# Attention and eight experts on one core: the rows beyond 512 of each expert as 64-column products inside the long ones, 64 more behind one branch, output transfers without an order between them

## The chip, the cores and the metric

One core of a Trainium2 chip runs the whole program in one launch. The metric is device time in microseconds (us): the median of the runs, each of them the time of one launch. Engines are named as in the profile: PE (TensorE matmul) and PEld (its weight loads), DVE (VectorE), ACT (ScalarE), POOL (GpSimd), SP (SyncE, which issues transfers).

## What is computed

Causal attention with a decay bias over 8 x 8 heads (576 positions, head size 64), and behind it a layer of eight experts with top-1 routing over the 8 x 576 = 4608 rows of 512 values that the attention leaves:

```python
scores = scale * q @ k.T + np.minimum(-(cum[:, None] - cum[None, :]), 0.0)   # causal
x = softmax(scores) @ v                       # per head, laid out as (4608, 512)
logits = (x / |x|) @ (emb / |emb|).T / tau
expert_idx = np.argmax(logits, axis=1)
for e in range(8):
    mask = expert_idx == e
    h = np.maximum(x[mask] @ w1[e], 0.0)      # 512 -> 1024
    out[mask] = gate_w[mask, None] * (h @ w2[e])   # 1024 -> 512
```

How many rows an expert has is known only on the chip; the mean is 576. Products are made from f16 pairs (a high and a low part), three products for one: high x high, high x low, low x high.

## The kernel before

The attention is laid out by hand in steps `step(n)` and ends some 395 us into the span; what the change touches comes after. Every engine runs its instructions in the order in which the program writes them (`manual_schedule`), so the code's order is the order of each queue.

Rows are routed by an indirect scatter into one list for each expert (`xs` in DRAM); an expert handles up to 640 of them here (`CAP`), in five tiles of 128. `MAIN` is 512 (four tiles), `HALF` is 576. Rows beyond 640 go to the loop `overflow`, which a count on the chip turns 0 times where there are none.

An expert e is worked off in two layers (the loop from line 1235 on):

- Layer 1, `l1(m, e, 0, MAIN)` for eight blocks m of 128 hidden units: 12 products of 512 columns each (`l1mm`, line 830; four parts c of the 512 inputs, three pairs k of high and low) into a tile `pxs` in PSUM, of which there are two, taken in turn. `hsplit` (lines 835 and 836) then makes the f16 pair: ACT writes the high part, DVE the low one.
- The tail of layer 1, `l1tail` (line 865): the fifth tile of rows. `cases` (line 859) writes two blocks of PE instructions, one behind "over 576 rows" (96 products of 128 columns) and one behind "513 to 576 rows" (96 products of 64 columns). Both write the PSUM tile `T`, and one `hsplit` over 128 x 1024 values follows.
- Layer 2, `l2(e, t)` for the four full tiles t: 24 products of 512 columns (line 913) into a `pxs`, then `put` (line 918): DVE scales the result into one of three slots of `Kx` (line 921), and POOL scatters it to `out` with an indirect transfer (line 922). In the last expert the last tile goes to the tile `om` instead (`l2h`) and is written behind the overflow loop (lines 1389 to 1391).
- The tail of layer 2, `l2tail` (line 876), third of the five turns t of the loop: again two blocks. Over 576 rows: 24 products of 512 columns into `Y` (line 880). From 513 to 576: 96 products of 64 columns with the weights as the loaded operand, whose result stands turned in `yT` (line 886). ACT copies `yT` to a slot of `Kx` (line 889). In the fifth turn `l2tail_out` (line 891) turns it back by four transposes behind a third branch, and `put` scatters `Y`.

Beside this, ACT and DVE convert the next weights (`wcv`: lines 814 and 822; `wsq`, line 786, takes their squares; `wnorm`, lines 797 to 804, makes the scale, with one product of 8 columns on PE), POOL gathers the next rows (`xload`, line 713), and `xprep` (lines 744 to 753) turns them: for experts 0 and 1 by four PE transposes (line 746) into the single PSUM tile `pxm`, which ACT (line 751) and DVE (line 753) read; from expert 2 on by transfers from SP.

Expert 0 is special: 384 of its rows are done early, its tiles 3 and 4 in two halves `hb` of four blocks each, and the rows of expert 1 are prepared between. `count1` loads an expert's row count into PE registers for the branches, twice in each expert (one for each case).

The output transfers all write `out`, so each waits until the one before has landed.

Of the kernel before, what the change touches and what calls it, by code (L numbers as in the profile page):

```python
# [12 lines left out]
I32 = mybir.dt.int32  # L13
# [96 lines left out]
def main(ctx, tc, qkh, qkc, vtin, s_in, emb, tau, w1h, w2h, out, shared, nb):  # L110
# [98 lines left out]
    def setup4():  # L209
# [14 lines left out]
        IX["e0"], IX["nf"], IX["ni"] = t[:, 470:470 + NE], t[:, 478:478 + NE], t[:, 486:486 + 2 * NE].bitcast(I32)  # L224
# [355 lines left out]
    def router(b, xt):  # L580
# [57 lines left out]
        def rows():  # L638
# [4 lines left out]
            nc.vector.tensor_copy(IX["ni"][:, 0:NE], IX["nf"])  # L643
            nc.vector.scalar_tensor_tensor(IX["ni"][:, NE:2 * NE], IX["nf"], float(HALF), IX["nf"], op0=ALU.is_le, op1=ALU.mult)
# [201 lines left out]
    def count1(e):  # L846
        for k in range(2):
            X[("n", e, k)] = nc.values_load(IX["ni"][0:1, NE * k + e:NE * k + e + 1], engines=[mybir.EngineType.PE], min_val=0, max_val=NT,
                                            skip_runtime_bounds_check_because="it is a count of the 4608 rows")

    def tails():
        ta, tb = (ps_t.tile([128, 2, 512], F32, tag="t", name=f"T{i}") for i in range(2))
        HT["T"] = ta.rearrange("p b (m t) -> p (b m) t", t=128)
        HT["Y"], HT["yT"] = tb[:, 0], tb[:, 1].rearrange("p (d t) -> p d t", d=4)
        z = PLs[0][:, 1600:1664].unsqueeze(1).to_broadcast([128, 8, 64])
        for o in (ta[:, 0], ta[:, 1], tb[:, 0], tb[:, 1]):
# [15 lines left out]
    def prods(m, e):  # L872
        (wH, wL), (hH, hL) = wt(2, m), (X[("T", e)][:, k, m] for k in range(2))
        return [(hH, wH, m == 0, False), (hL, wH, False, False), (hH, wL, False, m == 7)]

    def l2tail(e):
        def direct():
            for m in range(8):
                for h, w, a, z in prods(m, e):
                    nc.tensor.matmul(HT["Y"], h, w, start=a, stop=z)  # L880

        def turned():
            for d in range(4):
                for m in range(8):
                    for h, w, a, z in prods(m, e):
                        nc.tensor.matmul(HT["yT"][:, d, 0:64], w[:, 128 * d:128 * d + 128], h[:, 0:64], start=a, stop=z)
        cases(e, direct, turned)
        X[("y", e)] = yslot()[:, 0:256].rearrange("p (d t) -> p d t", d=4)
        nc.scalar.copy(X[("y", e)], HT["yT"][:, :, 0:64])

    def l2tail_out(e):
        with tc.If(X[("n", e, 1)] > MAIN):
            for d in range(4):
                nc.tensor.transpose(out=HT["Y"][0:64, 128 * d:128 * d + 128], in_=X[("y", e)][:, d], identity=ident)
        put(e, NTL - 1, HT["Y"])
# [5 lines left out]
    def l2h(e, t):  # L901
        for m in range(8):
            (wH, wL), (hH, hL) = wt(2, m), htile(m)
            for k, (h, w) in enumerate(((hH, wH), (hL, wH), (hH, wL))):
                nc.tensor.matmul(om, h[:, 128 * t:128 * t + 128], w, start=(m == 0 and k == 0), stop=(m == 7 and k == 2))

    def l2(e, t, mid={}):
# [517 lines left out]
```

## Time and profile before

| | |
|---|---|
| median of 3 runs | 789.34 us (787.21 to 792.22) |
| the profiled execution's own time | 790.14 us |
| span of its profile, first to last instruction | 788.0 us |
| mean granted PE clock | 0.989 of full |
| PE / ACT / DVE / POOL busy | 753.6 / 569.0 / 525.1 / 385.7 us |

A span is measured on the core itself; the execution's own time lies 2.1 us above it. In the profile a PE product's shown duration holds its way through the array as well, and products overlap: what one costs is the distance from its start to the start of the next. "Idle before" is the time in which an engine did nothing before an instruction, with what ended it; PEq is PE's sequencer, which runs the branches.

### The profile page before, as it was taken

The page shows a single profiled execution, that of the slowest core. Times are in us where ns is not written, and L with a number is a line of the kernel's source. Part 1 is how long each engine was busy: PE and PEld are TensorE (multiplying, and loading weights), DVE is VectorE, ACT ScalarE, POOL GpSimd, SP SyncE. Part 2 cuts the span into 40 slices and gives each one's busy share as a digit, 9 for nine tenths or more (in the row PEclk, how much of TensorE's full clock was granted, in tenths as well). Part 3 has the DMA queues.
Part 4 walks back from the last instruction along what each step waited for, and adds up shares of the span by engine and source line. Part 5 has one row for each costly group of instructions (what it writes and reads, how often), then busy time and mean ns, then how long its engine had stood idle before and what let it go on. Part 6 is the DMA issues. An engine that isn't in the chain of part 4 may idle for free. (4 is left out here: it accounts for less than half of the span.)

```text
span 788.0 us, 20375 instructions
## 1 busy us (share of the span) xinstructions
PE 753.6 (96%) x7694; PEld 537.2 (68%) x7694; DVE 525.1 (67%) x1789; ACT 569.0 (72%) x1020; POOL 385.7 (49%) x370
## 2 busy tenths in 40 slices
PE   8799999999999999998899999999999999999995
PEld 4599999999999999985465555545445555454452
DVE  7667888888888888877657757555575566644611
ACT  6689989999999998975638778647648586574500
POOL 8667798989898979771432112131131122211001
PEclk9899999999999999999999999999999999999998
DMA  8997879898979796780625756545555567642001
GB/s 157 193 196 134 177 177 208 179 204 181 203 177 210 175 209 152 183 280 20 225 77 177 190 169 193 144 147 163 144 197 133 148 195 172 207 98 79 15 28 42
DMA packets 76910, 125.26 MB, mean 159 GB/s; under 512 B 38960, under 2 KB 39364, under 8 KB 75934
## 3 DMA queue, kind: packets, MB, share of 16 engines
q0 software_dynamic: 20240, 70.92, 38.4%
q1 hardware_dynamic: 56560, 52.84, 24.7%
q8 instruction: 72, 1.18, 0.6%
q14 instruction: 38, 0.31, 0.1%
HBM read 95.23 MB, written 21.49 MB: 148 GB/s over the span
## 5 line engine op out<-in xcount | busy, mean ns | idle before, releaser
L240 POOL TENSOR_TENSOR PL<-P 128x576 f16<-128x576 f32 (+2 forms) x128 | 203.5, 1695 | 18.6 <-ACT P L483 10.5
L830 PEld LDWEIGHTS <-wt 128*128 128x128 f16 x1632 | 113.5, 98 | 93.7 <-issue 9.8
L922 POOL DMA_INDIRECT out<-Kx,xj x39 | 43.4, 1112 | 204.7 <-DVE Kx L921 153.2
L830 PE MATMUL pxs<-xH,wt 128*128 128x512 f16 (+1 forms) x512 | 141.6, 359 | 0.6 <-DVE hq L836 0.2
L511 PE MATMUL om<-vh,P 128*128 128x73 f16 x960 | 107.6, 199 | 3.4 <-DVE xt L536 3.0
L513 PE MATMUL om<-vh,PL 128*128 128x73 f16 x960 | 106.9, 198 | 0.5 <-POOL PL L240 0.5
L512 PE MATMUL om<-vl,P 128*128 128x72 f16 x960 | 107.0, 197 | 0.0
L348 PE MATMUL s<-qkb 96*128 96x288 f32 (+4 forms) x270 | 97.7, 375 | 1.6 <-DVE M L356 0.9
L512 PEld LDWEIGHTS <-P 128*128 128x128 bf16 x960 | 95.1, 99 | 4.5 <-issue 4.1
L513 PEld LDWEIGHTS <-PL 128*128 128x128 f16 x960 | 94.2, 98 | 0.6 <-POOL PL L240 0.6
L511 PEld LDWEIGHTS <-P 128*128 128x128 bf16 x960 | 94.1, 99 | 0.2
L713 POOL DMA_INDIRECT Qx<-xs,idx x40 | 43.2, 1080 | 102.9 <-ACT vjunk L786 50.9
L830 PE MATMUL pxs<-xL,wt 128*128 128x512 f16 (+1 forms) x256 | 90.3, 359 | 0.0
L356 DVE CUSTOM_DVE_ANT_0 junk<-s,mS 128x320 bf16<-128x320 f32 (+3 forms) x142 | 73.3, 524 | 4.9 <-PE s L348 3.5
L913 PE MATMUL pxs<-wt,hp 128*128 128x512 f16 x270 | 73.0, 379 | 0.0
L913 PE MATMUL pxs<-wt,hq 128*128 128x512 f16 x270 | 68.2, 379 | 0.0
L486 ACT ACTIVATE P<-tb 128x1024 f32<-128x1024 f32 x64 | 65.2, 1019 | 3.4 <-PE tb L453 2.3
L822 DVE SCALAR_TENSOR_TENSOR wt<-ring,idx,wt 128x512 f16<-128x512 f32 x80 | 56.8, 746 | 14.3 <-ACT wt L814 14.2
L921 DVE TENSOR_SCALAR Kx<-pxs,xj,idx 128x512 f32<-128x512 f32 x31 | 25.1, 810 | 61.6 <-PE pxs L913 37.0
L450 PE MATMUL tb<-QC,KC 128*128 128x448 f32 (+3 forms) x256 | 64.1, 309 | 0.0
L814 ACT ACTIVATE wt<-ring,idx 128x512 f16<-128x512 f32 x80 | 53.5, 711 | 14.0 <-DVE idx L801 14.0
L483 ACT ACTIVATE P<-ta 128x576 f32<-128x576 f32 x64 | 41.2, 644 | 28.2 <-PE ta L450 26.5
(268 smaller groups left out, 1903.0 us busy)
## 6 DMA issues: line engine op xcount, KB each, us to landing
qkb<-qkh POOLq DMA_DIRECT2D x15, 1216.0 KB, 9.3
ring<-w2h SPq DMA_DIRECT2D x44, 256.0 KB
ring<-w1h SPq DMA_DIRECT2D x36, 256.0 KB
vT<-vtin SPq DMA_DIRECT2D x28, 320.0 KB
KC<-qkh POOLq DMA_DIRECT2D x15, 576.0 KB, 8.9
QC<-qkh POOLq DMA_DIRECT2D x15, 576.0 KB, 8.1
rw<-w1h SPq DMA_DIRECT2D x15, 256.0 KB
rw<-w2h SPq DMA_DIRECT2D x12, 256.0 KB
```

The lines of the kernel that those rows point to most:

```text
L240: nc.gpsimd.tensor_tensor(out, a, b_, op=ALU.subtract)
L348: nc.tensor.matmul(out, G[g]["QB"][0:96, h, 128 * i:128 * i + 128], G[g]["KB"][0:96, h, lo:hi], start=True, stop=True)
L356: nc.vector.tensor_tensor_reduce(out=jk, in0=src, in1=ms, scale=1.0, scalar=NEG, op0=ALU.add, op1=ALU.max, accum_out=MP[n // 2][:, n % 2, ...
L450: nc.tensor.matmul(out, HD[n]["KC"][:, ks:ks + 128], HD[n]["QC"][:, qlo:qhi], start=False, stop=stop)
L486: nc.scalar.activation(HD[n]["P32"][:, 576:1600], HD[n]["tb"], AF.Exp, scale=0.125)
L511: nc.tensor.matmul(out, lh, vh[:, kb], start=(kb == 0), stop=False)
L512: nc.tensor.matmul(out[:, u:u + 72], lh, vl[:, kb], start=False, stop=False)
L513: nc.tensor.matmul(out, ll, vh[:, kb], start=False, stop=(kb == j))
L814: nc.scalar.activation(h, a, AF.Copy, scale=s)
L822: nc.vector.scalar_tensor_tensor(l, a, s, h, op0=ALU.mult, op1=ALU.subtract)
L830: nc.tensor.matmul(h, w[:, 128 * c:128 * c + 128], x[:, c, lo:hi], start=(c == 0 and k == 0), stop=(c == 3 and k == 2))
L913: nc.tensor.matmul(y, h, w, start=(m == 0 and k == 0), stop=(m == 7 and k == 2))
```

## The change

Expert by expert the fifth tile is split at row 576. The 64 rows from 512 on are always done: in layer 1 each 512-column product is followed by a 64-column product with the same weights into `T`; in layer 2 the turned products (12 of 64 columns) follow each block m of the second turn. The 64 rows from 576 on stand behind one branch in each layer (96 products of 64 columns each). The turned result is 128 columns wide for every expert, and four transposes bring it back into a `pxs`, without a branch. In expert 0, where there is no such turn, the eight groups of turned products follow `l2(0, 3)`; the transposes of expert 1's rows 3 and 4 move to other places of `l2(0, 3)`. The count is loaded once. The output transfers are declared independent of one another.

```diff
-    def l1mm(h, m, e, lo, hi, mid=None):
+    def l1mm(h, m, e, lo, hi, mid=None, tail=False):
...
-                nc.tensor.matmul(h, w[:, 128 * c:128 * c + 128], x[:, c, lo:hi], start=(c == 0 and k == 0), stop=(c == 3 and k == 2))
+                for o, a, b in ((h, lo, hi), (HT["T"][:, m, 0:64], MAIN, HALF)) if tail else ((h, lo, hi),):
+                    nc.tensor.matmul(o, w[:, 128 * c:128 * c + 128], x[:, c, a:b], start=(c == 0 and k == 0), stop=(c == 3 and k == 2))
...
-        l1mm(h, m, e, lo, hi, mid)
+        l1mm(h, m, e, lo, hi, mid, e > 0)
...
-    def cases(e, both, one):
-        with tc.If(X[("n", e, 0)] > HALF):
-            both()
-        with tc.If(X[("n", e, 1)] > MAIN):
-            one()
-
     def l1tail(e):
-        def go(n):
+        with tc.If(X[("n", e)] > HALF):
             for m in range(8):
-                l1mm(HT["T"][:, m, 0:n], m, e, MAIN, MAIN + n)
-        cases(e, partial(go, 128), partial(go, 64))
+                l1mm(HT["T"][:, m, 64:128], m, e, HALF, CAP)
         hsplit(*(X[("T", e)][:, k] for k in range(2)), HT["T"])
...
+    def turned(e, m, lo):
+        for d in range(4):
+            for h, w, a, z in prods(m, e, "T"):
+                nc.tensor.matmul(HT["yT"][:, d, lo:lo + 64], w[:, 128 * d:128 * d + 128], h[:, lo:lo + 64], start=a and d == 0, stop=z and d == 3)
+
     def l2tail(e):
...
-        cases(e, direct, turned)
-        X[("y", e)] = yslot()[:, 0:256].rearrange("p (d t) -> p d t", d=4)
-        nc.scalar.copy(X[("y", e)], HT["yT"][:, :, 0:64])
+        with tc.If(X[("n", e)] > HALF):
+            for m in range(8):
+                turned(e, m, 64)
+        X[("y", e)] = yslot()
+        nc.scalar.copy(X[("y", e)].rearrange("p (d t) -> p d t", d=4), HT["yT"])
 
     def l2tail_out(e):
-        with tc.If(X[("n", e, 1)] > MAIN):
-            for d in range(4):
-                nc.tensor.transpose(out=HT["Y"][0:64, 128 * d:128 * d + 128], in_=X[("y", e)][:, d], identity=ident)
-        put(e, NTL - 1, HT["Y"])
+        y = pxs()
+        for d in range(4):
+            nc.tensor.transpose(out=y[:, 128 * d:128 * d + 128], in_=X[("y", e)][:, 128 * d:128 * d + 128], identity=ident)
+        put(e, NTL - 1, y)
...
+            if tail:
+                turned(e, m, 0)
...
+    puts = []
...
+        for o in puts:
+            tc.declare_no_dep(ins, o, reason="a token is a row of one tile, so the tiles write distinct rows")
+        puts.append(ins)
...
-            l1mm(hb[:, m % 4], m, 0, SPL, MAIN)
+            l1mm(hb[:, m % 4], m, 0, SPL, MAIN, tail=True)
...
-    l2(0, 3, {3: lambda: xprep(1, 3, pxm())})
+    l2(0, 3, {1: lambda: xprep(1, 3, pxm()), 6: lambda: xprep(1, 4, pxm())})
...
+    for m in range(8):
+        turned(0, m, 0)
     l2tail(0)
...
                 l2tail_out(0)
-                xprep(1, 4, pxm())
...
-            if t == 4:
-                l2tail_out(e)
             if t == 2:
                 l2tail(e)
+            elif t == 4:
+                l2tail_out(e)
+                (l2 if nx else l2h)(e, LAST)
             else:
-                (l2 if nx or t < 4 else l2h)(e, t - (t > 2))
+                l2(e, t - (t > 2), tail=(t == 1))
```

Three places show what this does to the queues. The first is PE in the fifth turn of expert 2, between the end of layer 2's tile 2 and the start of tile 3 (`hv` is a block of hidden values, `Kx` the copied turned result, `om` the product of `wnorm`; what an instruction waits for stands in brackets).

```order
L913 MATMUL pxs<-wt,hv 128x512
L797 LDWEIGHTS onesb [waits DVE_49]
L797 MATMUL om<-idx,onesb 128x8 [waits Activation_49]
L892 COMPARE_AND_BRANCH
L894 MATMUL T_7484<-ident,Kx 64x128 x4
L892 UNCONDITIONAL_BRANCH
L892 UNCONDITIONAL_BRANCH [waits PE_49]
L913 LDWEIGHTS hv
L913 MATMUL pxs<-wt,hv 128x512 [waits DVE_49]
```

```order
L905 MATMUL pxs<-wt,hv 128x512
L796 LDWEIGHTS onesb [waits DVE_49]
L796 MATMUL om<-idx,onesb 128x8 [waits Activation_49]
L889 MATMUL pxs<-ident,Kx 128x128 [waits DVE_49]
L889 MATMUL pxs<-ident,Kx 128x128 x3
L905 LDWEIGHTS hv
L905 MATMUL pxs<-wt,hv 128x512 [waits DVE_49]
```

Above is before, below after: the branch is gone, and the transposes now write a `pxs`, so that one tile of the two is taken between two long products.

The second is PE in `l2(0, 3)` of expert 0, where rows of expert 1 are turned into `pxm` (`Qx` are gathered rows; of runs of equal rows the first or last is shown).

```order
L797 MATMUL om<-idx,onesb 128x8
L913 LDWEIGHTS xH [waits Activation_49]
...
L913 MATMUL pxs<-wt,xH 128x512
L746 MATMUL pxm<-ident,Qx 128x128 [waits DMASW0_49,DVE_49]
L746 MATMUL pxm<-ident,Qx 128x128 x3
L913 LDWEIGHTS xH [waits Activation_49]
...
L913 MATMUL pxs<-wt,xH 128x512
L860 COMPARE_AND_BRANCH
```

```order
L796 MATMUL om<-idx,onesb 128x8
L905 LDWEIGHTS xH [waits Activation_49]
...
L745 MATMUL pxm<-ident,Qx 128x128 [waits DMASW0_49,DVE_49]
L745 MATMUL pxm<-ident,Qx 128x128 x3
...
L905 LDWEIGHTS xH [waits Activation_49]
...
L745 MATMUL pxm<-ident,Qx 128x128 [waits DMASW1_49,DVE_49]
L745 MATMUL pxm<-ident,Qx 128x128 x3
...
L877 MATMUL yT<-xH,wt 128x64 [waits Activation_49]
```

Before, four transposes stand behind 12 of the 24 long products; after, four behind 6 of them and four more behind 21, and both groups write the one tile `pxm`.

The third is POOL's queue at the end of the program, the last expert's four output transfers.

```order
L922 DMA out<-Kx,xj 4608x512 [waits DMASW7_49,DMASW0_49,DVE_49]
...
L922 DMA out<-Kx,xj 4608x512 [waits DMASW1_49,DMASW0_49,DVE_49]
...
L922 DMA out<-Kx,xj 4608x512 [waits DMASW2_49,DMASW1_49,DVE_49]
L922 DMA out<-Kx,xj 4608x512 [waits DMASW2_49,DVE_49]
L1318 COMPARE_AND_BRANCH
L1318 ISA [waits DMASW4_49,DMASW5_49,DMASW3_49,DMASW6_49,DMASW2_49,DMASW7_49,DMASW1_49,DMASW0_49]
```

```order
L918 DMA out<-Kx,xj 4608x512 [waits DMASW0_49,DVE_49]
...
L918 DMA out<-Kx,xj 4608x512 [waits DMASW1_49,DVE_49]
L918 DMA out<-Kx,xj 4608x512 [waits DMASW2_49,DVE_49]
L918 DMA out<-Kx,xj 4608x512 [waits DMASW3_49,DVE_49]
L1319 COMPARE_AND_BRANCH
L1319 ISA [waits DMASW4_49,DMASW5_49,DMASW3_49,DMASW6_49,DMASW2_49,DMASW7_49,DMASW1_49,DMASW0_49]
```

The wait for the transfer just before (DMASW0, DMASW1, DMASW2) is gone; the wait for all transfers ahead of the overflow loop stays.

## Rows read from the trace of the kernel before

**Rows 1.** The page, part 1: busy time of each engine, its share of the span and its instructions.

```profile
PE 753.6 (96%) x7694; PEld 537.2 (68%) x7694; DVE 525.1 (67%) x1789; ACT 569.0 (72%) x1020; POOL 385.7 (49%) x370
```

**Rows 2.** Busy time by stage: from the second part of expert 0, experts 3 and 4 (columns: the stretch in us, its length, then busy us and instructions of PE, PEld, DVE, ACT and POOL, granted PE clock, DMA share, GB/s).

```profile
395.50:421.40 25.90, 23.53 (x356) 17.44 (x354) 15.21 (x46) 14.36 (x34) 7.17 (x7) 1.00 0.34 108
...
521.90:575.10 53.20, 52.67 (x316) 26.45 (x315) 29.82 (x74) 33.44 (x78) 11.18 (x10) 1.00 0.53 155
575.10:623.85 48.75, 48.02 (x392) 24.68 (x391) 29.87 (x74) 33.28 (x78) 11.46 (x10) 1.00 0.64 172
```

**Rows 3.** PE in order of time in layer 2 of expert 4 (start us, us, instruction, count, idle before and its releaser).

```profile
604.52 0.17 PE L797 MATMUL om<-idx,onesb 128*128 128x8 bf16 x1
604.55 0.81 PE L913 MATMUL pxs<-wt,hv 128*128 128x512 f16 x3
...
609.08 0.81 PE L913 MATMUL pxs<-wt,hv 128*128 128x512 f16 x3
610.21 2.97 PE L886 MATMUL T<-xH,wt 128*128 128x64 f16 x96 [0.32 <-PEq L860]
613.01 0.81 PE L913 MATMUL pxs<-wt,hv 128*128 128x512 f16 x3
...
618.22 0.60 PE L894 MATMUL T<-ident,Kx 128*64 128x128 f32 x4
618.66 0.59 PE L913 MATMUL pxs<-wt,hv 128*128 128x512 f16 x2
```

**Rows 4.** PE in order of time in expert 3: a load of counts (between the two products of 532.05), the tail of layer 1 (542.84 to 548.14), the tail of layer 2 (558.89), the start of its fifth turn.

```profile
532.05 0.81 PE L830 MATMUL pxs<-xH,wt 128*128 128x512 f16 x2
...
542.84 0.22 PE L830 MATMUL T<-xH,wt 128*128 128x128 f16 x1
...
548.14 0.22 PE L830 MATMUL T<-xH,wt 128*128 128x128 f16 x1
548.51 0.38 PE L913 MATMUL pxs<-wt,hv 128*128 128x512 f16 x1
...
558.89 5.34 PE L880 MATMUL T<-wt,xH 128*128 128x512 f16 x24
564.38 0.38 PE L913 MATMUL pxs<-wt,hv 128*128 128x512 f16 x1
...
569.56 0.17 PE L797 MATMUL om<-idx,onesb 128*128 128x8 bf16 x1
569.91 0.59 PE L913 MATMUL pxs<-wt,hv 128*128 128x512 f16 x2 [0.18 <-PEq L892]
```

**Rows 5.** DVE in order of time in the fifth turn of expert 3: `put` of tile 2 and of the fifth tile.

```profile
569.76 0.81 DVE L921 TENSOR_SCALAR Kx<-pxs,xj,idx 128x512 f32<-128x512 f32 x1 [2.96 <-PE om L797]
...
572.84 0.81 DVE L921 TENSOR_SCALAR Kx<-T,xj,idx 128x512 f32<-128x512 f32 x1
```

**Rows 6.** PE in order of time in the second part of expert 0 and at the start of expert 1.

```profile
396.91 0.22 PE L830 MATMUL pxs<-xH,wt 128*128 128x128 f16 x1
...
406.16 0.23 PE L830 MATMUL T<-xH,wt 128*128 128x64 f16 x2 [0.94 <-issue]
...
411.13 0.66 PE L746 MATMUL pxm<-ident,Qx 128*128 128x128 f32 x4 [0.20 <-DVE xL L753]
...
421.39 0.38 PE L830 MATMUL pxs<-xH,wt 128*128 128x512 f16 x1
```

**Rows 7.** ACT in order of time in the same stretch: the split of `T`, the first weight conversion, the first reading of `pxm` for expert 1's rows 3.

```profile
407.89 1.02 ACT L835 ACTIVATE xH<-T 128x1024 f16<-128x1024 f32 x1 [3.70 <-PE T L830]
...
412.43 0.72 ACT L814 ACTIVATE wt<-ring,idx 128x512 f16<-128x512 f32 x1 [2.43 <-DVE idx L801]
...
416.40 0.57 ACT L751 CAST xH<-pxm 128x512 f16<-128x512 f32 x1
```

**Rows 8.** DVE in order of time there: the last reading of `pxm` for expert 1's rows 1 and 3, the split of expert 1's first block.

```profile
410.40 0.68 DVE L753 TENSOR_TENSOR xL<-pxm,xH 128x512 f16<-128x512 f32 x1
...
417.00 0.69 DVE L753 TENSOR_TENSOR xL<-pxm,xH 128x512 f16<-128x512 f32 x1 [1.42 <-ACT xH L751]
...
420.97 0.69 DVE L836 SCALAR_TENSOR_TENSOR hv<-pxs,hv 128x512 f16<-128x512 f32 x1 [0.58 <-ACT hv L835]
```

**Rows 9.** The waits of PE from 395 to 780 us (who waited for whom: us in total, times, the longest).

```profile
PE om L797 <- ACT idx L788: 0.6, 1, 0.6
```

**Rows 10.** The chain that ended last (start us, us, what).

```profile
758.84 22.60 DMA out<-Kx,xj
781.44 0.10 POOLq L1318
```

**Rows 11.** POOL in order of time at the end: the output transfers of tile 2 and of the fifth tile.

```profile
774.69 0.97 POOL L922 DMA_INDIRECT out<-Kx,xj  x1 [9.70 <-DVE Kx L921]
778.18 0.97 POOL L922 DMA_INDIRECT out<-Kx,xj  x1 [2.52 <-DMA out<-Kx,xj]
```

**Rows 12.** DVE at the end: `put` of the fifth tile.

```profile
774.33 0.80 DVE L921 TENSOR_SCALAR Kx<-T,xj,idx 128x512 f32<-128x512 f32 x1
```

**Rows 13.** The page, part 5: all weight loads of line 830 (busy us, mean ns of one, idle before).

```profile
L830 PEld LDWEIGHTS <-wt 128*128 128x128 f16 x1632 | 113.5, 98 | 93.7 <-issue 9.8
```

**Rows 14.** Two stretches at the end of the attention, columns as in the second group.

```profile
355.00:360.00 5.00, 2.64 (x33) 1.70 (x30) 4.31 (x7) 1.83 (x7) 2.48 (x4) 1.00 0.06 18
360.00:365.00 5.00, 4.76 (x56) 3.64 (x56) 3.46 (x8) 3.85 (x10) 0.00 (x0) 0.66 0.00 0
```

More of the change, by code (lines that the diff above doesn't have):

```diff
@@ L846, in count1 @@
     def count1(e):
-        for k in range(2):
-            X[("n", e, k)] = nc.values_load(IX["ni"][0:1, NE * k + e:NE * k + e + 1], engines=[mybir.EngineType.PE], min_val=0, max_val=NT,
-                                            skip_runtime_bounds_check_because="it is a count of the 4608 rows")
+        X[("n", e)] = nc.values_load(IX["ni"][0:1, e:e + 1], engines=[mybir.EngineType.PE], min_val=0, max_val=NT,
+                                     skip_runtime_bounds_check_because="it is a count of the 4608 rows")
@@ L851, in tails @@
     def tails():
-        ta, tb = (ps_t.tile([128, 2, 512], F32, tag="t", name=f"T{i}") for i in range(2))
+        ta, tb = (ps_t.tile([128, 2, 512], F32, tag="t", name=n) for n in ("T", "yT"))
         HT["T"] = ta.rearrange("p b (m t) -> p (b m) t", t=128)
-        HT["Y"], HT["yT"] = tb[:, 0], tb[:, 1].rearrange("p (d t) -> p d t", d=4)
+        HT["yT"] = tb[:, 0].rearrange("p (d t) -> p d t", d=4)
         z = PLs[0][:, 1600:1664].unsqueeze(1).to_broadcast([128, 8, 64])
-        for o in (ta[:, 0], ta[:, 1], tb[:, 0], tb[:, 1]):
+        for o in (ta[:, 0], ta[:, 1], tb[:, 0]):
@@ L870, in l1tail, with prods @@
         hsplit(*(X[("T", e)][:, k] for k in range(2)), HT["T"])
-    def prods(m, e):
-        (wH, wL), (hH, hL) = wt(2, m), (X[("T", e)][:, k, m] for k in range(2))
+    def prods(m, e, t):
+        (wH, wL), (hH, hL) = wt(2, m), htile(m)
+        if t == "T":
+            hH, hL = (X[("T", e)][:, k, m] for k in range(2))
+        elif (e, t) == (0, 3):
+            hH, hL = (X[("T", 1)][:, k, m] for k in range(2))
+        else:
+            hH, hL = hH[:, 128 * t:128 * t + 128], hL[:, 128 * t:128 * t + 128]
@@ L882, in turned @@
-        def turned():
-            for d in range(4):
-                for m in range(8):
-                    for h, w, a, z in prods(m, e):
-                        nc.tensor.matmul(HT["yT"][:, d, 0:64], w[:, 128 * d:128 * d + 128], h[:, 0:64], start=a, stop=z)
-        cases(e, direct, turned)
-        X[("y", e)] = yslot()[:, 0:256].rearrange("p (d t) -> p d t", d=4)
-        nc.scalar.copy(X[("y", e)], HT["yT"][:, :, 0:64])
+                turned(e, m, 64)
+        X[("y", e)] = yslot()
+        nc.scalar.copy(X[("y", e)].rearrange("p (d t) -> p d t", d=4), HT["yT"])
@@ L902, in l2h, with l2 @@
         for m in range(8):
[L903 to L907, printed above, removed]
+            for h, w, a, z in prods(m, e, t):
+                nc.tensor.matmul(om, h, w, start=a, stop=z)
+    def l2(e, t, mid={}, tail=False):
         y = pxs()
         for m in range(8):
-            wH, wL = wt(2, m)
-            hH, hL = (h[:, 128 * t:128 * t + 128] for h in htile(m)) if (e, t) != (0, 3) else (X[("T", 1)][:, k, m] for k in range(2))
-            for k, (h, w) in enumerate(((hH, wH), (hL, wH), (hH, wL))):
-                nc.tensor.matmul(y, h, w, start=(m == 0 and k == 0), stop=(m == 7 and k == 2))
+            for h, w, a, z in prods(m, e, t):
+                nc.tensor.matmul(y, h, w, start=a, stop=z)
+            if tail:
+                turned(e, m, 0)
             if m in mid:
@@ L921, in put @@
         nc.vector.tensor_scalar(ys, y, xf[3], IX["RS"][:, 2 * e + 1:2 * e + 2], op0=ALU.mult, op1=ALU.mult)
[L922 to L923 removed]
+        ins = nc.gpsimd.indirect_dma_start(out=out, out_offset=bass.IndirectOffsetOnAxis(ap=xf[0].bitcast(U32), axis=0),
+                                           in_=ys, in_offset=None, bounds_check=NT - 1, oob_is_err=False).ins
+        for o in puts:
+            tc.declare_no_dep(ins, o, reason="a token is a row of one tile, so the tiles write distinct rows")
+        puts.append(ins)
     tasks, scats, mq, aq = deque(), deque(), deque(), deque()
```

11 lines of the change are left out of this document (2 added, 9 removed).

## The prediction

> **What bounds the kernel.** The page comes first: PE is busy 753.6 of 788.0 us [rows 1]. That is a mean over two halves, so the second view is busy time by stage. In experts 3 and 4 PE works 52.67 of 53.20 and 48.02 of 48.75 us while ACT, the next busiest, has 33; in the second part of expert 0 it works only 23.53 of 25.90 [rows 2]. So from 421 to 779 us a microsecond more or less in PE's queue is one in the total, and before that PE also waits. The third view, PE in order of time, gives what an instruction costs as the distance between starts: a 512-column product 216 ns, and 96 products of 64 columns with a load each 613.01 - 610.21 = 2.80 us, 29.2 ns apiece [rows 3]. The 96 products of 128 columns take 548.51 - 542.84 = 5.67 us [rows 4]. Which block ran tells how many rows an expert had: 3 ran the blocks for over 576 rows [rows 4], 4 those for 513 to 576 [rows 3], and in the same way 2, 6, 7 go with 3, and 0, 1, 5 with 4. No expert is below 513, so "576 rows always" adds no product that was left out before. Last comes the chain that ended the span: it holds the output transfers until 781.44, though PE was done at 779.1 [rows 10].
>
> **Term 1: experts over 576 rows (2, 3, 6, 7).** Before: 5.67 for the tail of layer 1, 564.38 - 558.89 = 5.49 for that of layer 2, 569.91 - 569.56 = 0.35 where the branch jumps past the transposes [rows 4], together 11.51 us. The first two hold 0.3 each in which the other block is jumped over: the last 128-column product starts at 548.14 and the next instruction 0.37 later, not 0.06. After: four trains of 96 short products, 4 x 2.80, and four transposes, 618.66 - 618.22 = 0.44 [rows 3], and nothing is jumped over: 11.64. That is +0.13 each, +0.5 in all. Two of the four trains no longer run as trains: in layer 1 each short product stands between two long ones. The nearest row for that is the 8-column product at 604.52 between 512-column ones: 0.03 later the next one starts [rows 3]. So I take 29 ns there too; the lower bound is 64 columns at 2.4 GHz, 27 ns, and the upper one is an unhidden load, a rival below.
>
> **Term 2: experts with 513 to 576 rows (1, 4, 5).** The same 192 short products and four transposes as before, and two blocks jumped over, as before: at 609.08 three long products take 0.65, and the short ones start 0.48 later [rows 3]. I take 0; if the jump is as short as the 0.3 above, 0.2 each are gained.
>
> **Term 3: the count.** One load of a register instead of two in seven experts: two products take 0.81 around the loads [rows 4] and 0.59 elsewhere [rows 3], so both loads together cost 0.2. I take half back, -0.7 in all (bounds 0 and -1.5).
>
> **Term 4: a new wait in the fifth turn.** `l2(e, 3)` used to write the `pxs` that was read two products earlier. Now the transposes take that one, and `l2(e, 3)` needs the tile of `l2(e, 2)`, which ended only 0.44 us before. DVE starts reading it at 569.76 and takes 0.81, to 570.57 [rows 5]; PE would be at its next product at 569.56 + 0.03 + 0.44 = 570.03. It stands 0.6 us, in experts 1 to 6 (in 7 the product goes to `om`): +3.5 us. Bounds: 0, if the tile were free in time, and 1.0 each if DVE is in a weight conversion then; at 569.76 it had been idle for 2.96. Behind the waiting product stand only PE's own instructions. `put` of the fifth tile then runs beside the product.
>
> **Term 5: expert 0's rows for expert 1.** Here PE meets the single tile `pxm`. PE from 396.91 [rows 6] has both halves of layer 1 with their short products, 96 x (56 + 29) ns = 8.2, a set of transposes between them, 0.44, and one jump, 0.4: 406.0. A stop of 0.94 in a train of short products [rows 6] and a second jump are gone from its way; a new stop of this kind is in the bounds. The reading of `pxm` is bound to ACT and DVE, whose chain begins with the split of `T`: 407.89 now, 406.0 then. From there the same instructions follow: `pxm` is read out 411.08 - 407.89 = 3.2 us later, and after the weight conversions a second time at 417.69, 9.8 us later [rows 7, 8]. PE has one more set of transposes, asks for it after 6 long products, at 407.7, and gets it at 409.2; 15 products later, at 412.9, it asks again and gets it at 415.8. That is 1.5 + 2.9 us of waiting in place of the 0.4 that 411.13 shows. Then 0.44 of transposes, three products, the turned train 2.80, a jump, expert 1's first block with its short products 2.94, and the transposes of expert 0's fifth tile, which take a `pxs`: 423.5. The next block waits for the split of the block just ended, ACT 0.6 and DVE 0.69 [rows 8], so it starts at 424.7 where it now starts at 421.39 [rows 6]: +3.3 us. Bounds: with no wait anywhere this stretch gets 2.1 shorter; with another 1 us stop and a slower clock it gets 6 longer. Expert 1 gives back 0.6: its `wnorm` now waits that long for ACT [rows 9], which gains time on a later PE.
>
> **Term 6: the end.** The last two output transfers start at 774.69 and 778.18, the second only when the first has landed [rows 11]; it lands 3 us later and frees the overflow loop at 781.44 [rows 10]. DVE has the fifth tile ready at 775.13 [rows 12]. Without the wait its transfer starts at 776.0 and has landed by 779, when PE's last product ends too, 0.1 later than now. The loop starts near 779.4, and what follows it is unchanged: -2.1 us. Bounds: 0, and -2.4, where PE's end binds. The other output transfers wait on POOL, where nothing that PE needs is queued in time of need: 0.
>
> **Sum.** 0.5 + 0 - 0.7 + 3.5 + 3.3 - 0.6 - 2.1 = +3.9 us. Against the profiled execution's own 790.14 that is 794.0; that execution lies 0.8 above the median of the runs, 789.34, so I forecast 793.2 us.
>
> **Rivals.** (a) The new waits don't come: DVE and ACT are ahead, PE runs through. Then term 4 is 0 and term 5 is -2.1: 0.5 - 0.7 - 2.1 - 0.6 - 2.1 = -5.0, 784.3 us. For it speaks DVE's idle time before its reading [rows 5]; against it, that the reading cannot start before the product it reads has ended. (b) The transfers' freedom does nothing: the loop waits for all of them anyway, and two at once may land later. Term 6 is 0, 795.3 us. Against it: 2.5 us of POOL's wait was for the first transfer alone [rows 11]. (c) The waits in expert 0 bring the clock down. In 355 to 360 us PE was busy 2.64 of 5 us, and in the next five the granted clock was 0.66 on average, that is 1.2 GHz for most of it [rows 14]: 3.4 us at half speed, +1.7, 794.9 us. The Trainium skill ("TensorE: Matmul & The Clock Gate", Part 1) says the same, that idleness drops the clock to its lower level; here its rule and these rows agree. (d) Slower: a short product between long ones cannot hide the weight load that follows it. A load shows 98 ns [rows 13]; if those stand in the open, each of the 768 short products of layer 1 costs 69 ns more, 53 us, 846 us, and from 10 ns each the change is slower by over 1%. Against it stand 96 loads in a row at 29.2 ns [rows 3]. The Trainium skill ("TensorE: Matmul & The Clock Gate", under "LDWEIGHTS (loading the stationary operand)") gives the loaded columns over 1.2 in ns, 107 ns for 128. By that alone every short product would cost 107 ns, and layer 1 some 60 us more; the trace differs, and the measurement decides.
>
> **How the numbers follow.** One per cent, 7.9 us, is about what a measurement of this kernel can tell from no change. Forecast 0.55, (a) 0.14, (b) 0.10, (c) 0.15, (d) 0.06. The forecast's own spread is 2.5 us to each side from term 5, and 1.5 from the others. Half of (a) would reach faster by over 1%, should more of the jumps go than I count: 0.07. Slower by over 1%: (d), and the upper ends of (b) and (c) where they meet, 0.08: 0.14. Within 1%: 0.79. The range reaches from between (a) and the forecast, 786.5, to 798.5, where (c) meets the upper bound of term 5.
>
> **What would show it.** In the changed kernel's profile: pairs of a long and a short product 245 ns apart (100 or more says (d)); PE idle 0.6 us behind the transposes in the fifth turn, released by DVE line 917; two waits of PE for `pxm` in expert 0, 1.5 and 2.9; the last output transfers 1.3 us apart and the overflow loop within 0.5 us of PE's end. Wrong it is if the experts from 2 on each take more than 1.5 us longer or are shorter than before, or if the granted clock falls between 406 and 425 us for longer than 4 us.

## The result and the profile after

The changed kernel takes 798.23 us (median of 7 runs, 795.13 to 799.33) against 789.34 (7 runs, 787.21 to 792.22): ratio 1.0104, 95% interval 1.0081 to 1.0126. It is 8.9 us slower, where 3.9 were forecast: inside the range, the sign right, the size wrong. The profiled execution has a span of 795.2 us. Part 1 of its page, to be read beside [rows 1]:

```profile
PE 759.4 (95%) x8765; PEld 554.8 (70%) x8765; DVE 526.8 (66%) x1788; ACT 569.7 (72%) x1020; POOL 382.8 (48%) x370
```

DVE, ACT and POOL are as busy as they were. So the search goes by stage. The next view of the changed kernel is busy time by stretch: second part of expert 0, expert 1 (from its second block of layer 1 on), expert 3, expert 4, and two short stretches inside the first two (columns as in [rows 2]).

```profile
395.40:425.30 29.90, 24.26 (x362) 19.05 (x361) 16.02 (x51) 16.11 (x38) 4.37 (x4) 0.94 0.32 101
425.30:476.90 51.60, 48.03 (x367) 24.02 (x367) 31.92 (x86) 36.51 (x86) 11.18 (x12) 0.93 0.68 165
530.60:584.40 53.80, 53.40 (x584) 30.40 (x583) 30.04 (x74) 33.43 (x78) 10.64 (x10) 1.00 0.62 155
584.40:633.10 48.70, 48.13 (x391) 24.82 (x390) 29.99 (x74) 33.32 (x78) 10.70 (x10) 1.00 0.69 170
...
416.50:419.90 3.40, 3.40 (x70) 3.40 (x67) 3.27 (x5) 3.01 (x7) 1.28 (x1) 0.50 0.10 30
...
467.70:474.50 6.80, 5.49 (x13) 1.93 (x13) 3.40 (x5) 5.19 (x15) 1.94 (x2) 0.50 0.74 239
```

The same view of the kernel before, for the stretches that answer to the first two:

```profile
396.50:421.40 24.90, 22.53 (x351) 16.99 (x350) 14.52 (x46) 14.36 (x34) 6.46 (x6) 1.00 0.35 113
421.40:468.70 47.30, 45.73 (x381) 23.58 (x379) 33.08 (x91) 37.67 (x91) 10.41 (x11) 1.00 0.70 191
```

The second part of expert 0 is 5.0 us longer, expert 1 4.3; experts 3 and 4, which stand for 2 to 7, are 0.6 longer and equal [rows 2]. In both long stretches the granted clock falls to 0.50 (1.2 GHz) once, as the two short stretches show. The end, from PE's last product to the end of the span, is 2.5 us shorter (6.4 instead of 8.9). So nearly all of the loss lies in 80 us in which PE is not the only bound.

PE of the changed kernel in order of time, in the second part of expert 0, in expert 1's fourth and fifth turn, and in expert 3 (layer 1 and fifth turn), beside [rows 3, 4, 6]:

```profile
405.40 1.46 PE L905 MATMUL pxs<-wt,xH 128*128 128x512 f16 x6
408.45 0.65 PE L745 MATMUL pxm<-ident,Qx 128*128 128x128 f32 x4 [1.59 <-DVE xL L752]
408.94 3.40 PE L905 MATMUL pxs<-wt,xH 128*128 128x512 f16 x15
415.06 0.65 PE L745 MATMUL pxm<-ident,Qx 128*128 128x128 f32 x4 [2.72 <-DVE xL L752]
...
416.20 4.51 PE L877 MATMUL yT<-xH,wt 128*128 128x64 f16 x96
420.86 0.38 PE L830 MATMUL pxs<-xH,wt 128*128 128x512 f16 x1
...
425.34 0.38 PE L830 MATMUL pxs<-xH,wt 128*128 128x512 f16 x1 [0.91 <-DVE hv L836]
...
459.47 0.17 PE L796 MATMUL om<-idx,onesb 128*128 128x8 bf16 x1
...
464.35 0.81 PE L905 MATMUL pxs<-wt,hv 128*128 128x512 f16 x3
465.56 0.66 PE L889 MATMUL pxs<-ident,Kx 128*128 128x128 f32 x4 [0.40 <-ACT Kx L884]
469.01 1.44 PE L905 MATMUL pxs<-wt,hv 128*128 128x512 f16 x3 [2.80 <-DVE Kx L917]
...
539.94 0.38 PE L830 MATMUL pxs<-xH,wt 128*128 128x512 f16 x1
540.16 0.19 PE L830 MATMUL T<-xH,wt 128*128 128x64 f16 x1
540.18 0.38 PE L830 MATMUL pxs<-xH,wt 128*128 128x512 f16 x1
...
578.14 0.63 PE L889 MATMUL pxs<-ident,Kx 128*128 128x128 f32 x4
579.18 0.81 PE L905 MATMUL pxs<-wt,hv 128*128 128x512 f16 x3 [0.41 <-DVE Kx L917]
```

A row "x3" or "x96" is a run of equal instructions. Three readings. In layer 1 a long product and its short one take 540.18 - 539.94 = 0.24 us: the interleaving costs what it should. In expert 3's fifth turn PE is next at 579.18, not at 578.61: the forecast wait, 0.57. In expert 1 the same wait is 2.96 us (466.05, which is 0.11 behind the start of the last transpose, to 469.01; the row's own 2.80 counts from that transpose's shown end). The products behind it run at half clock: "x3" takes 1.44, not 0.81.

Why the same wait is five times as long there can be read from DVE and ACT. First DVE of the changed kernel, expert 1's fourth and fifth turn; then ACT in the same stretch.

```profile
463.81 0.75 DVE L821 SCALAR_TENSOR_TENSOR wt<-Kx,idx,wt 128x512 f16<-128x512 f32 x1
466.16 0.75 DVE L821 SCALAR_TENSOR_TENSOR wt<-Qx,idx,wt 128x512 f16<-128x512 f32 x1 [1.61 <-ACT wt L813]
466.83 1.41 DVE L821 SCALAR_TENSOR_TENSOR wt<-ring,idx,wt 128x512 f16<-128x512 f32 x2
468.16 0.81 DVE L917 TENSOR_SCALAR Kx<-pxs,xj,idx 128x512 f32<-128x512 f32 x1
```

```profile
461.72 1.33 ACT L813 ACTIVATE wt<-rw,idx 128x512 f16<-128x512 f32 x2 [2.84 <-DVE idx L800]
...
464.94 0.56 ACT L884 COPY Kx<-yT 128x512 f32<-128x512 f32 x1
465.41 0.72 ACT L813 ACTIVATE wt<-Qx,idx 128x512 f16<-128x512 f32 x1
466.03 1.32 ACT L813 ACTIVATE wt<-ring,idx 128x512 f16<-128x512 f32 x2
```

PE ended `l2(1, 2)` at 465.2, but DVE reads that tile only at 468.16: its queue holds three conversions first. These wait for ACT's half of them, and ACT has worked without idle time since 461.72, where `wnorm`'s scale let it begin. `wnorm`'s product starts at 459.47. The same places in the kernel before, PE and then DVE:

```profile
454.56 0.17 PE L797 MATMUL om<-idx,onesb 128*128 128x8 bf16 x1
...
463.08 0.60 PE L894 MATMUL T<-ident,Kx 128*64 128x128 f32 x4
```

```profile
463.28 0.81 DVE L921 TENSOR_SCALAR Kx<-pxs,xj,idx 128x512 f32<-128x512 f32 x1
```

From `wnorm`'s product to DVE's reading it takes 8.72 us before and 8.69 after. In the kernel before, the product at 454.56 stood ahead of the turned train and of `l2(1, 2)`, 8.5 us of PE work, so the reading came just as PE had finished. The change moved 2.8 us of that work, the turned train, ahead of `wnorm`. PE became early, ACT and DVE did not.

POOL of the changed kernel at the end, beside [rows 11], and its chain that ended last, beside [rows 10]:

```profile
784.34 0.97 POOL L918 DMA_INDIRECT out<-Kx,xj  x1 [7.36 <-DVE Kx L917]
785.62 0.97 POOL L918 DMA_INDIRECT out<-Kx,xj  x1 [0.30 <-issue]
```

```profile
768.38 20.34 DMA out<-Kx,xj
...
788.72 0.10 POOLq L1319
```

The two last transfers are 1.28 us apart instead of 3.49, and the overflow loop starts at 788.72, 0.1 before PE ends (788.83); before it was 2.4 behind PE's end.

### The profile page after: what moved, and what is told of

Same layout as the page of the kernel before. It is cut to its first block, busy times and chain, and to the rows that moved or that the text cites. A ratio compares the mean times of both kernels' runs of the same rounds, so it can differ in the third digit from the quotient of the medians.

```text
span 795.2 us, 22464 instructions
## 1 busy us (share of the span) xinstructions
PE 759.4 (95%) x8765; PEld 554.8 (70%) x8765; DVE 526.8 (66%) x1788; ACT 569.7 (72%) x1020; POOL 382.8 (48%) x370
## 5 line engine op out<-in xcount | busy, mean ns | idle before, releaser
L830 PE MATMUL pxs<-xH,wt 128*128 128x512 f16 (+1 forms) x512 | 149.5, 360 | 1.1 <-DVE hv L836 0.9
L918 POOL DMA_INDIRECT out<-Kx,xj x39 | 41.7, 1069 | 183.7 <-DVE Kx L917 179.1
L830 PE MATMUL T<-xH,wt 128*128 128x64 f16 x768 | 105.9, 193 | 0.0
L830 PE MATMUL pxs<-xL,wt 128*128 128x512 f16 (+1 forms) x256 | 92.1, 360 | 0.0
L917 DVE TENSOR_SCALAR Kx<-pxs,xj,idx 128x512 f32<-128x512 f32 x39 | 31.4, 808 | 70.0 <-PE pxs L905 57.5
L905 PE MATMUL pxs<-wt,hq 128*128 128x512 f16 x270 | 70.3, 383 | 0.0
```

What stands on the lines that cost most here:

```text
L830: nc.tensor.matmul(o, w[:, 128 * c:128 * c + 128], x[:, c, a:b], start=(c == 0 and k == 0), stop=(c == 3 and k == 2))
L905: nc.tensor.matmul(y, h, w, start=a, stop=z)
```

## The experiments

Theory: the loss is waiting, not work. Expert 1's fifth turn costs some 6.2 us (2.96 of wait, 0.56 for ACT's copy, 2.7 at half clock), expert 0's two waits for `pxm` some 4.6 (1.76 and 2.88), the other fifth turns 0.43 to 0.57 each. Rivals: the interleaving itself, the clock alone, and that ACT and DVE pace the stretch, so that a wait taken away comes back behind. Kernels are compared by their ratio to the kernel before that ran beside them, since that kernel took 789.3, 791.2, 792.0 and 792.6 us in the four groups of runs.

**A bank of its own.** The fifth tile's transposes go to a PSUM bank that lay free, so `l2(e, 3)` finds its `pxs` free.

```diff
-        HT["yT"] = tb[:, 0].rearrange("p (d t) -> p d t", d=4)
+        HT["yT"], HT["Y"] = tb[:, 0].rearrange("p (d t) -> p d t", d=4), tb[:, 1]
...
-        y = pxs()
+        y = HT["Y"]
```

> The changed kernel, but the four transposes of the fifth tile write the PSUM bank that the change left free (the old place of Y) and no longer a pxs tile. Theory A (the time is lost in a few waits of PE: 2.96 us in expert 1's fifth turn and a half clock behind it that costs 2.6, 1.07 at the start of expert 1, 0.43 to 0.57 in experts 2 to 6): all of these go, -9 us against the changed kernel's 798.2, some 789; the waits for pxm in expert 0 (1.76 and 2.88) stay. Theory B (the time is lost in the products themselves, 1071 more of them and each with its load, and in the ACT and DVE work beside them): the waits move to the next product that needs a pxs, and the time falls by less than 2.5 us.

Measured: 788.04 us, ratio 0.9966 (0.9949 to 0.9983), that is 1.4% or about 11 us below the changed kernel, more than theory A's 9, and 0.3% below the kernel before. PE of this kernel in expert 1's fifth turn:

```profile
463.72 0.66 PE L889 MATMUL yT<-ident,Kx 128*128 128x128 f32 x4 [0.40 <-ACT Kx L884]
464.22 0.81 PE L905 MATMUL pxs<-wt,hv 128*128 128x512 f16 x3
```

The product behind the four transposes starts 0.50 after the first of them, with no wait. From the start of its layer 1 to that of expert 2, expert 1 is 6.7 us shorter (49.31 instead of 56.02); 2, 3 and 6 are 0.57 shorter each, 4 and 5 0.48; the half clock in expert 1 is gone, and so is the wait of 1.07 at its second block. The waits for `pxm` stay, 1.75 and 2.88. The Trainium skill ("Perfetto Trace Analysis", "Matmuls") asks that independent groups of products rotate through PSUM banks, so that one is read out beside the next group's products; here the trace agrees, 1.4% for one bank.

**DVE's queue alone.** Same PE order, same tiles; DVE's three conversions of expert 1's fourth turn stand behind the reading instead of ahead of it.

```diff
-                    wcv(2 if e > 1 else (0, 0, 3, 3, 2)[t])
+                    wcv(2 if e > 1 else (0, 0, 3, 3, 2)[t], hold=(e == 1 and t == 3))
...
+                if e == 1 and t == 3:
+                    wlow()
```

> The changed kernel, with one reordering on DVE: in expert 1's fourth turn DVE's three conversions of weights (0.75 us each) are issued behind the reading of the tile that PE's fifth turn waits for, no longer ahead of it. PE's order is the same. Theory A (PE's 2.96 us came from that reading standing in DVE's queue behind conversions that themselves waited for ACT): the reading starts within 0.3 us of the end of its product, PE's wait behind the transposes is 0.6 or less as in the other experts, the clock doesn't fall there, 5 us less than the changed kernel (798.2, ratio 1.0104): 792 to 794, ratio 1.004. Rival B (ACT is what paces this stretch; the wait moves to the next product that takes a converted weight, in the fifth turn or in expert 2's layer 1): the stretch of expert 1 is shorter by less than 2 us, ratio 1.008 or more.

Measured: 798.05 us, ratio 1.0069 (1.0045 to 1.0093), by the ratios about 2.8 us less than the changed kernel, though the two intervals overlap. DVE and PE of this kernel:

```profile
468.79 0.81 DVE L917 TENSOR_SCALAR Kx<-pxs,xj,idx 128x512 f32<-128x512 f32 x1 [0.64 <-PE pxs L905]
```

```profile
469.15 0.66 PE L889 MATMUL pxs<-ident,Kx 128*128 128x128 f32 x4 [0.40 <-ACT Kx L884]
469.65 0.81 PE L905 MATMUL pxs<-wt,hv 128*128 128x512 f16 x3
...
475.90 0.38 PE L830 MATMUL pxs<-xH,wt 128*128 128x512 f16 x1 [0.90 <-DVE Kx L917]
```

The trace shows the cause of the wait: one reordering on DVE takes the whole 2.96 us away, and the half clock with it. But the time gives back at most about half of theory A's 5 us. Expert 1's stretch, 51.45 instead of 56.02, already holds a new wait of 1.07 (475.90: the last tile's reading, now itself behind the conversions that were put off), which is rival B's part. A second, 0.89 in expert 2, has another cause: ACT starts the split of that expert's second block 7.52 us after the expert's start, where the changed kernel does so after 6.07. Why ACT stood there isn't known. Expert 0 is 1.1 longer in this profile, 1.0 of it at the jump behind its turned train (1.31 instead of 0.31).

**The train back in the third turn.** Expert 1's turned train behind `wnorm`'s product, as before.

```diff
     def l2tail(e):
+        for m in range(8 if e == 1 else 0):
+            turned(e, m, 0)
...
-                l2(e, t - (t > 2), tail=(t == 1))
+                l2(e, t - (t > 2), tail=(t == 1 and e > 1))
```

> The changed kernel, but in expert 1 alone the 96 turned short products stand as one train in the third turn, behind wnorm's product, and not in the second turn between the long ones. Theory A (the put of tile 2 is queued on DVE behind weight conversions that follow wnorm; from wnorm to the fifth turn PE now has 5.9 us of work where it had 8.5): the wait in expert 1's fifth turn falls from 2.96 to about 0.6, the wait of its transposes for ACT (0.56) goes, the granted clock no longer falls there; -5.5 us, some 792.7. Theory B (the wait comes of the pxs tile alone, whatever stands ahead): it stays near 3 us and the time within 1 us of 798.2.

Measured: 792.0 us, ratio 1.0021 (0.9999 to 1.0043), 0.8% below the changed kernel. PE of this kernel behind the transposes:

```profile
464.88 0.60 PE L891 MATMUL pxs<-ident,Kx 128*128 128x128 f32 x4
465.94 0.81 PE L907 MATMUL pxs<-wt,hv 128*128 128x512 f16 x3 [0.47 <-DVE Kx L919]
```

The wait is 0.63, near that of the other experts, the wait for ACT's copy is gone, and no half clock follows. With the run before it this shows both ends: DVE's reading is late, because PE's work ahead of it was moved. A new stop of 1.08 stands at the jump behind this train.

**The clock alone.** Eleven long products that nothing reads run in expert 0's second wait and in expert 1's fifth turn; PE stands as long, busy.

```diff
...
+    def warm(k):
+        for _ in range(k):
+            nc.tensor.matmul(HT["Y"], PLs[0][:, 0:128], PLs[0][:, 0:512], start=True, stop=True)
...
-    l2(0, 3, {1: lambda: xprep(1, 3, pxm()), 6: lambda: xprep(1, 4, pxm())})
+    l2(0, 3, {1: lambda: xprep(1, 3, pxm()), 6: lambda: (warm(11), xprep(1, 4, pxm()))})
...
+                if e == 1:
+                    warm(11)
```

> The changed kernel with 11 long products that nobody reads, into the free PSUM bank, put into two of PE's waits: ahead of the second set of transposes for pxm in expert 0 (a wait of 2.88 us) and ahead of the long products of expert 1's fifth turn (2.96 us); 2.4 us each, so neither wait gets longer. Theory A (the granted clock fell to 1.2 GHz behind these two waits because of them): PE goes on at the same moments, the clock stays at 2.4 GHz, 1.9 us come back in expert 0's turned train and 2.6 in expert 1: -4.5 us, some 793.7. Theory B (the clock falls there for another reason, such as the dense short products): it falls as before and the time stays within 1 us of 798.2.

Measured: 794.33 us, ratio 1.0049 (1.0028 to 1.0070): 0.55% or about 4.3 us of the change's loss is the clock, half of what it loses, and near theory A's 4.5. The granted clock is 1.00 throughout in expert 1 here, and that stretch 2.7 us shorter.

**The places of expert 0's transposes.** Back where they were; layer 1's short products of expert 1 as a train, since their rows are ready only there.

```diff
-    l2(0, 3, {1: lambda: xprep(1, 3, pxm()), 6: lambda: xprep(1, 4, pxm())})
+    l2(0, 3, {3: lambda: xprep(1, 3, pxm())})
...
                 l2tail_out(0)
+                xprep(1, 4, pxm())
...
-        l1mm(h, m, e, lo, hi, mid, e > 0)
+        l1mm(h, m, e, lo, hi, mid, e > 0 and not (e == 1))
...
+        for m in range(8 if e == 1 else 0):
+            l1mm(HT["T"][:, m, 0:64], m, e, MAIN, HALF)
```

> The changed kernel, with expert 0's two late transposes for expert 1 put back to the places that they had before (one behind the product of the fourth m, one behind expert 0's overflow rows) and layer 1's short products of expert 1 as a train behind the long ones, since their rows are then ready only there. Theory A (the waits of 1.76 and 2.88 us for pxm come from these places): neither is there any more, the second part of expert 0 is 4 to 5 us shorter, time 793 to 794.5, ratio 1.005. Rival B (the waits are bound to ACT and DVE, which stay as late as they were, so PE waits as long at the next place that takes their product, the split before expert 1's next block): the stretch to expert 1's next block is shorter by less than 1.5 us, time 797 or more. The wait of 2.96 in expert 1's fifth turn stays under both.

Measured: 794.12 us, ratio 1.0017 (0.9993 to 1.0042), 0.9% below the changed kernel. PE of this kernel:

```profile
410.93 0.66 PE L745 MATMUL pxm<-ident,Qx 128*128 128x128 f32 x4 [0.30 <-DVE xL L752]
...
414.02 2.96 PE L879 MATMUL yT<-xH,wt 128*128 128x64 f16 x96
419.15 0.39 PE L830 MATMUL pxs<-xH,wt 128*128 128x512 f16 x1 [2.17 <-PEq L882]
```

The waits of 1.76 and 2.88 are one of 0.46, as theory A says. A new stop stands at the jump behind the turned train, 2.33 instead of 0.31, and behind it the clock falls, at the start of expert 1 (columns as in [rows 2]):

```profile
419.40:422.75 3.35, 3.35 (x10) 1.15 (x8) 0.80 (x2) 1.05 (x3) 0.38 (x1) 0.50 0.75 259
```

That is 1.7 us lost, and expert 1 is 1.7 longer. In this profile expert 0's and expert 1's stretch together are only 2.5 us shorter; but the profiled run, 798.07, is the slowest of its ten, and the timing says more (0.9%, its two intervals 0.25% to each side). What the places cost lies between these.

**Interleaving undone in layer 1**, experts 2 to 7:

```diff
-        l1mm(h, m, e, lo, hi, mid, e > 0)
+        l1mm(h, m, e, lo, hi, mid, e > 0 and not (e > 1))
...
+        for m in range(8 if e > 1 else 0):
+            l1mm(HT["T"][:, m, 0:64], m, e, MAIN, HALF)
```

> The changed kernel, with the 96 short products of layer 1 of experts 2 to 7 issued as one train behind the long ones, no longer one between each two long ones. Theory A (a short product costs 29 ns in either place): each of these experts within 0.3 us of the changed kernel, time within 1.5 us of it (798.2), ratio to the kernel before 1.009 to 1.012. Rival B (in the train the split of T's last rows comes later for PE, or the fifth turn has more work behind wnorm's product): fifth-turn waits of 0.55 unchanged. Rival C (a short product between long ones costs 10 ns more than in a train, its load not hidden): each of these six experts 1.0 us shorter, 792 us.

Measured: 803.82 us, ratio 1.0153 (1.0105 to 1.0202, 4 runs), 0.5% above the changed kernel with overlapping intervals: theory A's 1.5 us is missed to the other side, and rival C is refuted, since trains gain nothing. Beside the last kernel, in the same group of runs, experts 2, 3, 5, 6 and 7 are 0.2 to 0.6 longer and expert 4 is 1.7, 1.4 of them at one jump. What is regular is a stop of 0.2 in each expert, here PE in expert 3's layer 1:

```profile
542.99 0.80 PE L830 MATMUL pxs<-xH,wt 128*128 128x512 f16 x2
```

The same stop stands in the kernel before, at 532.05 [rows 4], where the caption and the prediction take it for the register loads of the count. It is a wait for a `pxs`: DVE reads that tile until 532.42, and PE goes on at 532.48. DVE of the kernel before:

```profile
531.74 0.68 DVE L836 SCALAR_TENSOR_TENSOR hq<-pxs,hq 128x512 f16<-128x512 f32 x1
```

The two loads (line 848) lie at 526.2 and 526.6, 0.30 us each, and the products beside them keep their 0.216. In the changed kernel the stop is not there: in expert 3 no distance in layer 1 exceeds its product by 0.06. A block of layer 1 takes 2.94 us in it and 2.59 in the other two kernels, so PE asks for that tile later. The interleaving thus gains 0.2 in each expert, by a wait that it covers and not by a load.

**The end alone, from both sides.** The kernel before with the transfers unordered, and the changed kernel with them in order (the first edit, and its reverse):

```diff
+        for o in puts:
+            tc.declare_no_dep(ins, o, reason="a token is a row of one tile, so the tiles write distinct rows")
+        puts.append(ins)
```

> The kernel before, with the output transfers unordered and nothing else changed. Theory A (the freedom of the last two transfers is worth what the end of the two profiles shows, 8.95 us from PE's last product to the end of the span before and 6.37 after; everything earlier is untouched): end 6.4 us, time 2.1 to 2.6 below the kernel before beside it, ratio 0.997. Rival B (the loop waits for both anyway, and two transfers at once land later): end 8.5 or more, ratio 1.000. Rival C (unordered transfers also free POOL earlier in the middle of the kernel, so that PE gains there): more than 4 us below, with PE's last product itself earlier by 1.5 or more after expert 1's start.

> The changed kernel without the declaration that the output transfers are independent: each waits for the one before to land. Theory A (the freedom is worth something at the end alone): the stretch from PE's last product to the end goes from 6.4 us back to some 9, all stretches before stay, +2.6 us, some 800.8. Theory B (it also frees POOL's gathers and so PE earlier on): +4 us or more, with new waits of PE in experts 0 and 1.

Measured: 790.11 us, ratio 0.9975 (0.9951 to 0.9999), and 799.7, ratio 1.0106 (1.0077 to 1.0134). The first is 2.0 us less, near theory A, its interval only just clear of 1; from PE's end to the end of its span are 6.9 us instead of 8.9. The second can't be told from the changed kernel by time, though its end is 8.6 instead of 6.4; from expert 0 on its profile has 3.4 us at half clock where that of the changed kernel has 10.2, so the two profiles aren't alike elsewhere (its profiled run, 795.77, is the fastest of its five by 3.6). POOL of the second:

```profile
780.89 0.97 POOL L918 DMA_INDIRECT out<-Kx,xj  x1 [7.36 <-DVE Kx L917]
784.38 0.97 POOL L918 DMA_INDIRECT out<-Kx,xj  x1 [2.52 <-DMA out<-Kx,xj]
```

It waits 2.52 again for the first transfer: the mechanism is shown, its price is some 2 us by the profiles and the first kernel's time.

**Versions that beat both.** The bank, the old places and the train in the third turn together; and the same without the third edit.

> The changed kernel with three edits together: the fifth tile's transposes go to a PSUM bank of their own, expert 1's turned train stays in the third turn, and expert 0's late transposes stand where they stood before (expert 1's short products of layer 1 as a train). Theory A (the two classes of waits are independent and add up): no wait of PE over 0.8 us from 396 to 780 us that the kernel before doesn't have, no stretch of half clock after 365 us, 4 to 5 us below the kernel with the bank alone (788.0): 783 to 784.5, ratio to the kernel before 0.990 to 0.993. Rival B (with the bank, the waits for pxm were already overlapped with what limits expert 1's first block, so that their removal gives under 1.5 us): 786.5 to 788, ratio 0.995 to 0.997.

> The fifth tile's transposes in a PSUM bank of their own and expert 0's late transposes in their former places, as in the version with three edits, but expert 1's turned train left where the change has it, in the second turn between the long products. Theory A (the stops that the version with three edits showed around the third turn, 0.41, 0.28 and 1.24 us, come from the turned train standing behind wnorm's product and from the jump there; with the bank alone that place cost 0.34 and 0.57): about 1 us below the version with three edits (787.9, ratio 0.993), ratio 0.991 to 0.993. Rival B (expert 1 is paced by ACT and DVE there, so PE waits as long somewhere else): ratio 0.993 to 0.995, the same sum of stops from 452 to 466 us, about 1.9.

Measured: 787.91 us, ratio 0.9934 (0.9908 to 0.9960) for three edits, 0.7% below the kernel before; between its theories, the gain over the bank alone being 0.3%, with overlapping intervals. The longest stops left in its profile are the jumps behind two turned trains, 1.45 us in expert 0 and 1.24 in expert 1. Without the third edit 790.38, ratio 0.9975 (0.9954 to 0.9996): worse, against both theories (the two intervals just overlap). In its profile expert 1 is 1.0 us shorter than with three edits (51.36 instead of 52.38), its stops from 452 to 466 us being 0.9 instead of 1.9, as theory A has it, but expert 2 is 2.0 longer. ACT and PE of that kernel in expert 2's layer 1, whose second block PE had done at 477.1:

```profile
479.60 0.60 ACT L835 ACTIVATE hp<-pxs 128x512 f16<-128x512 f32 x1 [4.39 <-remote]
```

```profile
480.97 0.38 PE L830 MATMUL pxs<-xH,wt 128*128 128x512 f16 x1 [0.89 <-DVE hp L836]
```

ACT stood 2.5 us beyond PE's end of the block, and for the releaser the profile names no instruction of another engine. It is the place of the late split in the run that reordered DVE, which ran beside this one; in the changed kernel and the seven others made from it ACT is there within 0.3 of PE. So the time of this run doesn't decide between its theories: in its profile, what it lost it lost to a stop of ACT whose cause stays open.

## Why the size was wrong, point by point

- **Terms 1 to 3.** Experts 2, 3 and 6 are 0.54 longer, 4 and 5 equal, 7 is 0.04 shorter. 0.24 for a pair of products is right, rival (d) is refuted. In term 2 the two jumps cost 0.31 each, not 0.48. Term 3 misread its row: the 0.2 at 532.05 is a wait for DVE, and the loads of the count show no cost. That wait is gone all the same, 0.2 in each expert, so the term came out at its bound by luck. Experts 2 to 7 are together 1.3 better than forecast.
- **Term 4, the step that failed.** In experts 2, 3 and 6 the wait is 0.57 as sized (0.6), in 4 and 5 0.43 and 0.48. The forecast took expert 3's row, where DVE had been idle for 2.96 us [rows 5], for all six, with 1.0 as the upper bound. Expert 1 has another schedule of conversions (three a turn, behind a `wnorm` in the third), and there the wait was 2.96, the copy 0.56 and the half clock 2.7 us. With the 0.6 that term 5 has expert 1 give back, the forecast for expert 1 was 0. That wait for ACT did go, but expert 1 took 4.2 in all. The rows to read were DVE and ACT in expert 1, not expert 3.
- **Term 5, expert 0.** The waits for `pxm` came as worked out, 1.76 and 2.88 for 1.5 and 2.9, and 1.07 for 1.2 at the split. The stretch is 5.06 longer, not 3.3, and most of the rest is rival (c): the 96 turned products at 416.20 take 4.35 us, not 2.80. Without the half clock little of this is gained (layer 1 to layer 1, 24.6 instead of 25.05 in the kernel with ordered transfers), since the jump behind the train then stands 1.40 instead of 0.31.
- **Term 6, the end.** 2.5 instead of 2.1 by the profiles; 2.0 by the time of the kernel before with this edit alone.
- **Rival (c)** had 0.15 and 1.7 us, at one place. It came at two, 3.4 us long in expert 0 and 6.8 in expert 1, and cost 4.3 by the run that kept PE busy. Rivals (a) and (b) did not come.
- **The sum.** Expert 0 +5.1, expert 1 +4.2, experts 2 to 7 +1.6, the end -2.5: +8.4 us from expert 0's second part on, which the changed kernel's profile reaches 1.1 earlier. The timed difference is 8.9. That it lies inside the range is partly luck: the upper end was set for a stop and a slow clock in expert 0, and half of the loss came from expert 1. The signs that the prediction named came (pairs 0.24 apart, 0.6 in expert 3's fifth turn, two waits for `pxm`, the transfers 1.28 apart), but none of them looks at expert 1.

## What to carry to other kernels

A new wait on a buffer is priced at the queue of the engine that frees it, and in every stage that has a queue of its own: the same tile was freed 0.43 to 0.57 us late in five experts and 2.96 in the one with another order on DVE. When work of the busiest engine is moved ahead of a step that feeds the others, ask what covered their latency before, and what the clock does behind the wait. A wait taken out by reordering the engine that frees the buffer can come back at the next buffer; one more buffer gave more than the reordering, 1.4% against some 0.35%.

## What the runs showed of the hardware

- Behind PE's wait of 2.96 us in expert 1 the granted clock fell to 0.50, that is 1.2 GHz, in all four profiles that have that wait (for 3.4 us in three, 6.8 in the changed kernel). Behind the 2.88 in expert 0 it fell in the changed kernel and the one that reorders DVE, and not in those with the bank, the train in the third turn, layer 1's trains or ordered transfers. It also fell behind the stop of 2.33 at a jump in the kernel with the old places. Waits of 0.57 never did it. The Trainium skill ("TensorE: Matmul & The Clock Gate", "A second HAM failure mode: psum-queue depth-cycling") reports a clock that goes up and down where PE is idle for very short times, often, between groups of products that cycle through PSUM banks. These traces don't show that: the short waits, once in each expert, left the clock at 1.00, and it fell behind long ones alone.
- A jump over a block costs PE 0.31 or 0.32 us in experts 1, 4 and 5 of the changed kernel, behind long products or interleaved ones. Behind the turned train of expert 0 it took 1.15 to 2.33 us in the nine kernels made from the changed one, and 0.31 in the changed one itself, most of whose train ran at half clock. The profile puts it down to PE's own sequencer; why it varies is open.
- PE stopped for 0.19 to 0.58 us inside trains of turned products in all six profiles of the last two groups of runs (792.0 and 792.6 us for the kernel before); in the first six profiles (789.3 and 791.2) no such stop is over 0.15. The kernel that reorders DVE has the PE order of the changed one and shows them, the changed kernel does not. What differs between the groups was not found; it is why ratios are used here.
